# An FFT convolution and an MLP on one core: row-tiled second DFT stage, an in-place product, data as weights in the inverse, layer norm 2 inside the MLP

## The chip, the cores and the metric

The kernel runs on one core of a Trainium2 chip. A core has a matrix engine (TensorE, PE in the profile; its weight loads are listed apart as PEld), a vector engine (VectorE, DVE), a scalar engine (ScalarE, ACT), a general one (GpSimd, POOL) and a queue engine (SyncE, SP) that issues most transfers. Matmul results go to PSUM; ACT and DVE move them to SBUF. The metric is the device time of one execution in microseconds (us).

## The reference, cut to what matters

The sequence has S = 2048 tokens and D = 512 channels, all arrays are bf16.

```python
qn   = layernorm(q)                                   # over the channels
kv   = (k convolved causally with 4 taps per channel) * v
y    = irfft(rfft(pad(kv)) * rfft(pad(ssm_k)))[:S]    # per channel, length 4096, float32
y    = bf16(y) + kv * ssm_D                           # skip term per channel
h    = q + qn * y                                     # gate
out  = h + relu(layernorm(h) @ w1) @ w2               # w1: 512 x 1376, w2: 1376 x 512
```

The long convolution is the costly part beside the MLP. With the padded transform the kernel computes odd frequencies alone, with two stages of DFT matrices (32 values of `k1`, then 64).

## The kernel before, in words

The order on every engine is that of the program text (`manual_schedule`); the waits follow from the tiles that an instruction reads and writes. Tiles live in pools, and a pool that takes over the place of another waits for it.

**Setup (L94 to L192).** SP loads the filter `sk`, then `kT` and `vT` in four chunks each with transposing DMAs (L110 to L113), so that channels lie on partitions. POOL and DVE make integer phases, and ACT makes sine tables of them (`_sin`, `table`): `cc`, `cs` and, by POOL, `cn` = -`cs`. These hold the second stage's DFT matrices of all 32 `k1` as 128 x 128 blocks in which two 64 x 64 blocks stand on the diagonal and the rest is zero.

**Stage 1 (`stage1`).** `to_rows` (L195) turns the time axis to the partitions with PE transposes. Then, for eight groups `gb` of channels, 64 pairs of a matmul with the high and the low part of the first stage's matrix run on four row groups of 32 partitions, and ACT and DVE copy the four results. For the filter (L268), two `taps` (L255: four matmuls against diagonal weights, and a DVE product with `vT`) follow each `gb`. For the data (L292, `wide=True`) most matmuls have 128 columns, of which 64 meet zeros. A pool of eight PSUM buffers serves all of these.

**Stage 2 (`stage2`, L226).** For each `k1`, four matmuls of 256 columns in fp32r, with the DFT block as weights. For the filter (L283) DVE adds `ssm_D` to the real part and ACT copies the imaginary part into `kf`.

**Product (L308 to L340).** For each of 16 pairs `kp` of `k1`, `product` runs stage 2 on the data into PSUM, ACT copies columns 176 to 255 to SBUF for POOL, and DVE and POOL multiply by both parts of `kf` (L321). Two steps later `finish` adds the four partial products with matmuls against +1 and -1 on the diagonal (L331), and ACT writes the sums over `kf` (L333).

**Inverse stage 1 (L389).** 64 steps `m`, each with two matmuls (L394) whose weights are 128 columns of the data in `kf` and whose 256 moving columns are `dre`/`dim`. In between `ec_turns` and `ec_sins` make the table `ecore`.

**Inverse stage 2 (`inv2`, L412).** For each quarter `q` of the tokens 128 small matmuls (L421) on 16 tiles of 32 x 32, weights from the table, data moving, in full fp32 (the trace has two instructions for each). ACT copies the result to `zt`.

**Layer norms, gate, MLP (L428 to L526).** `ln1(q)` normalizes the input tokens (`xh`); `gate` multiplies with `zt`, adds, and takes the statistics for layer norm 2; `hln_` applies it; `transposes` turns the result on PE, and ACT copies it to `hlnT` (L473). `mlp1(sc)` makes 44 matmuls (L485) of 512 columns with relu on ACT, `mlp2(sc)` 44 more (L498); DVE adds the residual (L501), and SP stores.

Of the kernel before, what the change touches and what calls it, by code (L numbers as in the profile page):

```python
# [15 lines left out]
P = 128  # L16
# [40 lines left out]
def kernel(  # L57
# [28 lines left out]
    slotA = pl.push("slotA")  # L86
    vp = pl.push("vp")
    early = pl.push("early")
    wp = pl.push("wp", side="right")
    kvp = pl.push("kvp", side="right")  # L90
# [7 lines left out]
    dtab = consts.tile([P, DC, 64], BF16, name="dtab")  # L98
    for dp in range(2):
        src = bass.AP(tensor=A_ssm_D.tensor, offset=A_ssm_D.offset + 64 * dp, ap=[[0, 64], [P, DC], [1, 64]])  # L100
        nc.scalar.dma_start(out=dtab[64 * dp:64 * dp + 64, :, :], in_=src)
    vT = vp.tile([P, DC, S], BF16, name="vT")
    CH = 512
    kT = [(kvp if c < 2 else early).tile([P, DC, CH + 16], BF16, name=f"kT{c}") for c in range(4)]
    wdiag = kvp.tile([P, DC, KS, P], BF16, name="wdiag")
# [15 lines left out]
    eps_t = consts.tile([P, 1], F32, name="eps_t")  # L121
    nc.vector.memset(eps_t[:], EPS)

    hsc = consts.tile([P, 2], F32, name="hsc")
    hbi = consts.tile([P, 2], F32, name="hbi")
    for t_, v_ in ((hsc, TURN / 8192), (hbi, -0.5 * TURN)):
        nc.vector.memset(t_[:], 0.0)
        for dp in range(2):
            nc.vector.memset(t_[halves[dp], dp:dp + 1], v_)
# [6 lines left out]
    n1i = early.tile([P, 1], I32, name="n1i")  # L136
    for s in range(0, P, 32):
        nc.gpsimd.iota(n1i[s:s + 32, :], pattern=[[0, 1]], base=0, channel_multiplier=1)
    r1 = early.tile([P, 32], I32, name="f1_r")
    nc.gpsimd.iota(r1[:], pattern=[[2, 32]], base=1, channel_multiplier=0)  # L140
    n2i = early.tile([P, 1], I32, name="n2i")
    for s in range(0, P, 64):
        nc.gpsimd.iota(n2i[s:s + 64, :], pattern=[[0, 1]], base=0, channel_multiplier=1)
    r2 = early.tile([P, 32, 64], I32, name="w_r")
    nc.gpsimd.iota(r2[:], pattern=[[2, 32], [128, 64]], base=1, channel_multiplier=0)
    r3 = early.tile([P, 64], I32, name="dm_r")
# [6 lines left out]
    n1c = early.tile([P, 1], F32, name="n1c")  # L153
    n2c = early.tile([P, 1], F32, name="n2c")
# [3 lines left out]
    t1 = early.tile([P, 64], I32, name="f1_t")  # L158
    _turns(nc, t1[:, 0:32], r1[:], n1c[:], 128, True)
    _turns(nc, t1[:, 32:64], r1[:], n1c[:], 128, False)  # L160
    f1f = early.tile([P, 64], F32, name="f1_f")
# [4 lines left out]
    cc = wp.tile([P, 32, P], F32R, name="c2c")  # L166
    cs = wp.tile([P, 32, P], F32R, name="c2s")
    cn = wp.tile([P, 32, P], F32R, name="c2n")
    tsn = early.tile([P, 32, 64], I32, name="w_ts")
    _turns(nc, tsn[:], r2[:], n2c[:], 8192, False)  # L170

    def table(dst, turns):
        for dp in range(2):
            nc.scalar.activation(out=dst[:, :, 64 * dp:64 * dp + 64], in_=turns[:], func=ACT.Sin,  # L174
                                 scale=hsc[:, dp:dp + 1], bias=hbi[:, dp:dp + 1])

    table(cs, tsn)
    f1hi = consts.tile([P, P], BF16, name="f1_hi")
    f1lo = consts.tile([P, P], BF16, name="f1_lo")
    for f in (f1hi, f1lo):  # L180
        nc.gpsimd.memset(f[:, 64:128], 0.0)
    nc.vector.tensor_copy(out=f1hi[:, 0:64], in_=f1f[:])
    f1d = early.tile([P, 64], F32, name="f1_d")
    nc.vector.tensor_tensor(out=f1d[:], in0=f1f[:], in1=f1hi[:, 0:64], op=ALU.subtract)
    nc.vector.tensor_copy(out=f1lo[:, 0:64], in_=f1d[:])
    _turns(nc, r2[:], r2[:], n2c[:], 8192, True)
    for rg in range(DC):
        nc.gpsimd.tensor_tensor(out=wdiag[:, rg, :, :], in0=ident[:].unsqueeze(1).to_broadcast([P, KS, P]),
                                in1=wsh[:, rg, :].unsqueeze(2).to_broadcast([P, KS, P]), op=ALU.mult)
    for h in range(4):  # L190
        hs = slice(8 * h, 8 * h + 8)
        nc.gpsimd.tensor_single_scalar(out=cn[:, hs, :], in_=cs[:, hs, :].bitcast(F32), scalar=-1.0, op=ALU.mult)  # L192


# [6 lines left out]
    def copy(eng, o, i):  # L201
        if eng == "A":
            nc.scalar.copy(out=o, in_=i)  # L203
        else:
            nc.vector.tensor_copy(out=o, in_=i)

    def stage1(fl, a_out, engs, between=None, wide=False):

        for gb in range(8):
            pss = [psum.tile([P, 8, 64], F32, tag="ps", name=f"ps1_{r}") for r in range(4)]  # L210
            for gi in range(8):
                for f, first in ((f1hi, True), (f1lo, False)):
                    for rg in range(4):
                        rows = slice(32 * rg, 32 * rg + 32)
                        w = 2 if wide and gi < 7 else 1
                        nc.tensor.matmul(out=pss[rg][:, gi:gi + w, :].rearrange("p g c -> p (g c)"),  # L216
                                         lhsT=fl[rows, 8 * gb + gi, :, :].rearrange("p d n -> p (d n)"),
                                         rhs=f[rows, 0:64 * w], start=first, stop=not first,
                                         tile_position=(32 * rg, 0), skip_group_check=wide)
            for rg in range(4):  # L220
                j0 = 64 * rg + 8 * gb
                copy(engs[(4 * gb + rg) % len(engs)], a_out[:, :, j0:j0 + 8], pss[rg][:].rearrange("p g c -> p c g"))
# [3 lines left out]
    def stage2(ps, a_in, kp, s):  # L226

# [55 lines left out]
    for kp in range(16):  # L283
        ks = slice(2 * kp, 2 * kp + 2)
        ps = [psum.tile([P, 2, 256], F32, tag="ps", name=f"ps2k{s}") for s in range(2)]
        for s in range(2):
            stage2(ps[s], a1k, kp, s)
# [47 lines left out]
    for kp in range(16):  # L335
        product(kp)
        if kp >= LAG:
            finish()
# [219 lines left out]
```

## Time and profile before

| | |
|---|---|
| time, median of three runs | 246.2 us (245.7 to 248.65) |
| span of the profiled execution | 244.7 us, first to last instruction |
| busy share | PE 86%, DVE 63%, PEld 59%, ACT 54%, POOL 27% |
| chain that ended last | PE 80%, ACT 9%, issue 4%, DMA 3%, DVE 2% |

The profile is that of one execution; the time of that very execution is not recorded apart, and the median lies 1.5 us above its span. A busy engine is one with an instruction in flight; matmuls overlap, so PE's busy share is no measure of how much of its peak it reaches. The chain names, step by step from the end, what the next instruction waited for. The granted clock is the share of TensorE's full clock; it was 0.968 in the mean.

### The profile page before, as it was taken

What the parts mean: (1) busy time and instruction counts of PE and PEld (TensorE: products, weight loads), DVE (VectorE), ACT (ScalarE), POOL (GpSimd) and SP (SyncE); (2) the same over time, 40 slices, a digit from 0 to 9 for tenths busy, and PEclk for the clock granted to TensorE, in tenths of its full rate; (3) what the DMA queues carried; (4) which work ended last, traced back from release to release, by engine and by line L of the source; (5) the groups of instructions that cost most, each with busy time, mean ns of one, the idle gap of its engine ahead of it and who ended that gap; (6) DMA issues with size and microseconds to landing.
All of it is one profiled execution on the core that took longest, in us unless ns stands there. A gap on an engine that the chain in (4) does not pass through costs nothing.

```text
span 244.7 us, 7171 instructions
## 1 busy us (share of the span) xinstructions
PE 209.5 (86%) x3088; PEld 144.7 (59%) x3104; DVE 153.1 (63%) x296; ACT 132.7 (54%) x232; POOL 65.3 (27%) x94
## 2 busy tenths in 40 slices
PE   0586998999857999989988786499999999999992
PEld 0573546999646999969975464334544544454440
DVE  7986987967636989959975778200247747751031
ACT  3878554666765888879943321636226136335500
POOL 6499600000004999971010221000002202200000
PEclk9999999999997999999999999559999999999998
DMA  6999910000000000039970000000110011012011
GB/s 211 302 202 168 144 34 3 4 0 0 5 3 5 1 0 0 3 74 209 279 250 3 5 5 5 0 0 0 30 48 11 0 44 46 0 34 56 0 43 43
DMA packets 23663, 13.88 MB, mean 57 GB/s; under 512 B 19056, under 2 KB 22480, under 8 KB 23504
## 3 DMA queue, kind: packets, MB, share of 16 engines
q1 hardware_dynamic: 22560, 13.36, 24.3%
q8 instruction: 24, 0.39, 0.7%
q10 hardware_dynamic: 1072, 0.07, 0.4%
q14 instruction: 7, 0.06, 0.1%
HBM read 7.08 MB, written 2.10 MB: 38 GB/s over the span
## 4 chain that ended last, share of the span: by engine, by line
PE 80%; ACT 9%; issue 4%; DMA 3%; DVE 2%; ACTq 0%
PE ps1m L485 17%; PE ps2m L498 15%; PE pz L421 9%; PE psi L394 6%; PE pst L198 5%; PE psy L331 5%; PE pkv L259 4%; PE ps L216 4%; PE u L231 4%; DMA sk<-in_A_ssm_k_dram 3%; PE u L233 3%; PE ps2k L233 3%; PE ps2k L231 3%; ACT a1x L203 2%; ACT c2c L174 2%
## 5 line engine op out<-in xcount | busy, mean ns | idle before, releaser
L485 PE MATMUL ps1m<-hlnT,w 128*128 128x512 bf16 (+1 forms) x175 | 41.2, 397 | 1.5 <-ACT hlnT L473 1.3
L487 ACT ACTIVATE h1T<-ps1m 128x512 bf16<-128x512 f32 (+1 forms) x44 | 26.2, 597 | 27.1 <-PE ps1m L485 27.1
L501 DVE TENSOR_TENSOR o<-ps2m,xh 128x512 bf16<-128x512 f32 x16 | 10.9, 690 | 47.9 <-PE ps2m L498 47.9
L498 PE MATMUL ps2m<-w,h1T 128*128 128x512 bf16 (+1 forms) x169 | 38.8, 379 | 0.4
L485 PEld LDWEIGHTS <-w 128*128 128x128 bf16 (+1 forms) x176 | 18.2, 104 | 24.0 <-issue 5.4
L321 DVE TENSOR_TENSOR t<-u,kf 128x704 fp32r<-128x704 f32 x32 | 26.8, 887 | 4.4 <-ACT usb L317 4.4
L321 POOL TENSOR_TENSOR t<-usb,kf 128x320 fp32r<-128x320 f32 x32 | 28.4, 927 | 3.0 <-ACT usb L317 2.4
L498 PEld LDWEIGHTS <-h1T 128*128 128x128 bf16 (+1 forms) x176 | 17.1, 98 | 20.0
L421 PE MATMUL pz<-bp,ecore 32*32 32x128 f32 x1024 | 22.0, 384 | 6.6 <-issue 5.7
L430 POOL TENSOR_SCALAR rstd<-mv 128x4 f32<-128x4 f32 x8 | 1.8, 229 | 92.2 <-DVE mv L437 92.2
L421 PEld LDWEIGHTS pz<-bp,ecore 32*32 32x32 f32 x1024 | 15.2, 103 | 13.2 <-issue 8.9
L425 ACT CAST zt<-pz 128x512 bf16<-128x512 f32 x16 | 8.2, 600 | 21.6 <-PE pz L421 21.6
L435 DVE BATCH_NORM_STATS2 st<-xh 128x6 f32<-128x512 bf16 x32 | 19.7, 683 | 0.0
L333 ACT CAST kf<-psy 128x512 fp32r<-128x512 f32 x32 | 18.4, 646 | 1.6
L394 PE MATMUL psi<-dre,kf 128*128 128x256 f32 x64 | 15.8, 287 | 0.8 <-ACT kf L333 0.8
L473 ACT COPY hlnT<-pt 128x1024 bf16<-128x1024 bf16 x8 | 7.7, 1015 | 15.0 <-PE pt L472 15.0
L331 PE MATMUL psy<-t,ipos 128*128 128x512 f32 x48 | 15.8, 390 | 0.0
L394 PE MATMUL psi<-dim,kf 128*128 128x256 f32 x64 | 15.4, 282 | 0.0
L259 PE MATMUL pkv<-kT,wdiag 128*128 128x512 bf16 x56 | 14.8, 381 | 0.4
L198 PE MATMUL pst<-ident,sk 128*128 128x128 bf16 x64 | 6.7, 295 | 9.1 <-DMA sk<-in_A_ssm_k_dram 9.1
L203 ACT CAST a1k<-ps 128x512 fp32r<-128x512 f32 x20 | 10.4, 593 | 7.1 <-PE ps L216 7.1
L289 ACT CAST kf<-ps2k 128x512 fp32r<-128x512 f32 x16 | 10.3, 641 | 5.4 <-PE ps2k L233 5.3
(107 smaller groups left out, 426.7 us busy)
## 6 DMA issues: line engine op xcount, KB each, us to landing
sk<-in_A_ssm_k_dram SPq DMA_DIRECT2D x1, 2048.0 KB, 8.3
xh<-in_A_q_dram SPq DMA_DIRECT2D x4, 512.0 KB, 8.4
out_dram<-o SPq DMA_DIRECT2D x64, 32.0 KB, 1.6
w<-in_B_w_dram SPq DMA_DIRECT2D x1, 1376.0 KB, 15.1
w<-in_B_w_dram SPq DMA_DIRECT2D x1, 1280.0 KB, 18.3
w<-in_B_w_dram SPq DMA_DIRECT2D x1, 96.0 KB, 17.9
dtab<-in_A_ssm_D_dram ACTq DMA_DIRECT2D x2, 32.0 KB, 8.3
kT<-in_A_k_dram SPq DMA_TRANSPOSE x4, 6.5
```

The lines of the kernel that those rows point to most:

```text
L198: nc.tensor.transpose(out=pst[:, i, :], in_=src[:, :, :, 8 * q + i], identity=ident[:])
L231: nc.tensor.matmul(out=ps[:, kk, :], lhsT=w_re[:, k1, :], rhs=a_in[:, k1, :], start=True, stop=False, skip_group_check=True)
L259: nc.tensor.matmul(out=ps[:], lhsT=wdiag[:, rg, j, :], rhs=kT[c][:, rg, 16 - j:CH + 16 - j], start=(j == 0), stop=(j == KS - 1))
L321: eng.tensor_tensor(out=t[:, :, j, :], in0=in0.unsqueeze(1).to_broadcast([P, 2, n, 2]), in1=kfr[:, :, j, ks], op=ALU.mult)
L331: nc.tensor.matmul(out=psy[:], lhsT=m_[:], rhs=t_.rearrange("p j k -> p (j k)"), start=first, stop=not first)
L333: nc.scalar.copy(out=kf[:, s, :, 2 * kp:2 * kp + 2], in_=psy[:].rearrange("p (j k) -> p j k", k=2))
L394: nc.tensor.matmul(out=ps[:, i, :], lhsT=kf[:, c, 4 * m:4 * m + 4, :].rearrange("p r k -> p (r k)"), rhs=d[:].rearrange("p a b -> p (a b)" ...
L421: nc.tensor.matmul(out=pz[32 * a:32 * a + 32, r4, l4, :], lhsT=ecore[rows, rho, n2, :], rhs=rhs, start=(rho == 0), stop=(rho == 1), tile_p ...
L435: nc.vector.bn_stats(out=st[:, i, :], in_=xh[:, 4 * q + i, :])
L485: nc.tensor.matmul(out=ps1[:fsz, :], lhsT=w1[:, c, fc * P:fc * P + fsz], rhs=hlnT[:, c, sc * SCW:(sc + 1) * SCW], start=(c == 0), stop=(c ...
L487: nc.scalar.activation(out=h1T[:fsz, fc, :], in_=ps1[:fsz, :], func=ACT.Relu)
L498: nc.tensor.matmul(out=ps2[:], lhsT=h1T[:ksz, fc, i * P:(i + 1) * P], rhs=w2[:ksz, fc, :], start=(fc == 0), stop=(fc == NFC - 1))
```

## The change

**Setup.** The tables become one tile `tab` of 64 x 64 blocks (sine, cosine, minus sine, minus cosine) on both halves of the partitions, without zeros: one ACT call each over 2048 elements, one ahead of the filter's transposes and three behind them. `cn` goes. `dsm` (four small loads), `sel` and `dx` are new; POOL makes `dx`.

**Stage 1.** The skip term is no longer added to `kf`: for the filter, `skip_term` begins each PSUM buffer with a matmul of two rows. The data's stage 1 is no longer widened and comes directly behind its transposes, ahead of stage 2 of the filter.

**Stage 2.** Each matmul takes a 64-row tile, with real and imaginary part together as 128 weight columns; the two halves of the partitions are two tiles (`tile_position`). The filter's result is copied over `a1k`.

**Product.** For the data both `u` and its rotation by 90 degrees are computed, so the complex product becomes two multiplications with the filter's values, written over `a1x` and `a1k`. DVE does 11 of 16 `kp` from PSUM, POOL five, for which ACT copies. The recombining matmuls go.

**Inverse stages.** Inverse stage 1 makes 16 steps `b` of 16 matmuls, 256 in all, each with 128 moving columns and 128 weight columns of data, and writes over `ax`. Inverse stage 2 takes the data as weights (32 rows, 128 columns) and 32 columns of the table as the moving part, in fp32r, so its result has channels on partitions.

**Layer norms and MLP.** The input and its normalized form are turned by transposing DMAs (`rows_T`), the gate works on the turned form, and its result feeds mlp1 directly. `w1c` is w1 less its column means, and the scale of layer norm 2 is applied with the residual on the output; `back` turns the gate's result back for the statistics and the residual.

The diff, cut to its core:

```diff
+    dsm = consts.tile([P, 64], BF16, name="dsm")
+    nc.gpsimd.memset(dsm[:], 0.0)
+    for rg in range(DC):
+        nc.scalar.dma_start(out=dsm[32 * rg:32 * rg + 2, :], in_=A_ssm_D[rg * P:(rg + 1) * P].rearrange("(d g) -> d g", d=2))
...
-    cc = wp.tile([P, 32, P], F32R, name="c2c")
-    cs = wp.tile([P, 32, P], F32R, name="c2s")
-    cn = wp.tile([P, 32, P], F32R, name="c2n")
+    tab = wp.tile([P, 32, 4, 64], F32R, name="tab")
...
+    nc.gpsimd.memset(dx[:], 0.0)
...
+    nc.gpsimd.tensor_copy(out=dx[:, :, 0:32], in_=dsm[:].unsqueeze(2).to_broadcast([P, 64, 32]))
+    _sin(tab[:, :, 0, :], tsn[:], 8192)
...
+    def skip_term(ps, rg, gb):
+        rows = slice(32 * rg, 32 * rg + 2)
+        nc.tensor.matmul(out=ps[:].rearrange("p g c -> p (g c)"), lhsT=sel[rows, :],
+                         rhs=dx[rows, 8 * gb:8 * gb + 8, :].rearrange("p g c -> p (g c)"),
+                         start=True, stop=False, tile_position=(32 * rg, 0), skip_group_check=True)
...
-    table(cc, r2)
+    _sin(tab[:, :, 1, :], r2[:], 8192)
+    _sin(tab[:, :, 2, :], tsn[:], 8192, neg=True)
+    _sin(tab[:, :, 3, :], r2[:], 8192, neg=True)
...
-    stage1(xfl, a1x, "ADADADAA", wide=True)
+    stage1(xfl, a1x, "ADADADAA")
...
+    prod = pl.push("prod", bufs=4, side="right")
+    psum = pl.push("psP", bufs=2, space=PSUM)
+    def stage2(ps, h, src, kp, w_re, w_im):
+        for kk in range(2):
+            k1 = 2 * kp + kk
+            for s, w in enumerate((w_re, w_im)):
+                for d in range(2):
+                    nc.tensor.matmul(out=ps[:, kk, d, h, :, :],
+                                     lhsT=tab[halves[d], k1, w:w + 2, :].rearrange("p a b -> p (a b)"),
+                                     rhs=src[halves[d], :, k1, s, :], start=(s == 0), stop=(s == 1),
+                                     tile_position=(64 * d, 0), skip_group_check=True)
...
+    for kq in range(8):
+        ps = psum.tile([P, 2, 2, 2, DC, 64], F32, tag="ps", name="psk")
+        for h in range(2):
+            stage2(ps, h, a1k, 2 * kq + h, 1, 0)
+        copy("A", pair(a1k, 2 * kq), half(ps, 0))
+        copy("D", pair(a1k, 2 * kq + 1), half(ps, 1))
+    for kp in range(16):
+        u = psum.tile([P, 2, 2, 2, DC, 64], F32, tag="ps", name="u")
+        stage2(u, 0, a1x, kp, 1, 0)
+        stage2(u, 1, a1x, kp, 2, 1)
+        eng, us = nc.vector, [half(u, 0), half(u, 1)]
+        if kp % 3 == 1:
+            eng = nc.gpsimd
+            for h in range(2):
+                usb = prod.tile([P, 4, DC, 64], F32, tag="usb", name="usb")
+                nc.scalar.copy(out=usb[:], in_=us[h])
+                us[h] = usb[:]
+        for h, dst in enumerate((a1x, a1k)):
+            eng.tensor_tensor(out=pair(dst, kp), in0=us[h], in1=pair(a1k, kp).bitcast(F32), op=ALU.mult)
...
+    def inv1(b):
+        ps = psum.tile([P, 8, P], F32, tag="ps", name="psi1")
+        d, g0 = b // 8, 8 * (b % 8)
+        for g in range(8):
+            for src, r, first in ((ax, ra, True), (ak, rb, False)):
+                nc.tensor.matmul(out=ps[:, g, :], lhsT=src[:, :, d, g0 + g],
+                                 rhs=r[:].rearrange("p a b -> p (a b)"), start=first, stop=not first)
+        copy("A" if b % 4 != 3 else "D", ax[:, :, d, g0:g0 + 8], ps[:].rearrange("p g x -> p x g"))
...
+    def rows_T(dst, src):
+        nc.sync.dma_start_transpose(out=dst[:].rearrange("p i r t -> p (i r) t"), in_=src.rearrange("p i d -> p (i d)"))
...
+    def inv2(q, pool):
+        pz = pool.tile([P, DC, 4, P], F32, tag="pz", name="pz")
+        for i in range(4):
+            for a in range(4):
+                n2 = 16 * a + 4 * q + i
+                for rho in range(2):
+                    for rg in range(DC):
+                        rows = slice(32 * rg, 32 * rg + 32)
+                        nc.tensor.matmul(out=pz[:, rg, i, 32 * a:32 * a + 32],
+                                         lhsT=ax[rows, 64 * rho + n2, :, :].rearrange("p d g -> p (d g)"),
+                                         rhs=ecore[rows, rho, n2, :], start=(rho == 0), stop=(rho == 1),
+                                         tile_position=(32 * rg, 0), skip_group_check=True)
+        return pz
+
+    def gate(q, pz):
+        for r in range(DC):
+            nc.vector.tensor_tensor(out=qT[q][:, :, r, :], in0=pz[:, r, :, :], in1=qT[q][:, :, r, :], op=ALU.mult)
+        nc.vector.tensor_tensor(out=xT[q][:], in0=qT[q][:], in1=xT[q][:], op=ALU.add)
+        hT[q] = xT[q]
+
+    def back(q):
+        nc.sync.dma_start_transpose(out=xh[:, 4 * q:4 * q + 4, :].rearrange("p i (r c) -> p (i r) c", r=DC),
+                                    in_=hT[q][:].rearrange("p i r t -> p (i r t)"))
...
-            nc.vector.tensor_tensor(out=o[:], in0=ps2[:], in1=xh[:, t, :], op=ALU.add)
+            nc.vector.scalar_tensor_tensor(out=o[:], in0=ps2[:], scalar=rstd2[:, t, :], in1=xh[:, t, :],
+                                           op0=ALU.mult, op1=ALU.add)
...
+    FS = 344
+    for n in range(DFF // FS):
+        fs = slice(n * FS, (n + 1) * FS)
+        pm = psB.tile([P, 512], F32, tag=f"pm{n}", name="pm")
+        for c in range(DC):
+            nc.tensor.matmul(out=pm[:, 0:FS], lhsT=ones[:], rhs=w1[:, c, fs], start=(c == 0), stop=(c == DC - 1))
+        nc.vector.tensor_tensor(out=w1c[:, :, fs], in0=w1[:, :, fs],
+                                in1=pm[:, 0:FS].unsqueeze(1).to_broadcast([P, DC, FS]), op=ALU.subtract)
+    pz0 = inv2(0, psA)
+    gate(0, pz0)
+    back(0)
...
+    pz1 = inv2(1, psB)
+    gate(1, pz1)
+    back(1)
+    pl.pop("psA")
+    psum = pl.push("psM", bufs=4, space=PSUM)
+    ln1(2)
+    stats(xh[:, 0:4, :], mv2, rstd2, 0)
+    mlp1(0)
+    pz = inv2(2, psB)
+    gate(2, pz)
+    back(2)
+    ln1(3)
+    mlp2(0)
+    stats(xh[:, 4:8, :], mv2, rstd2, 1)
+    mlp1(1)
+    pz = inv2(3, psB)
+    gate(3, pz)
+    back(3)
+    mlp2(1)
+    stats(xh[:, 8:12, :], mv2, rstd2, 2)
+    mlp1(2)
+    mlp2(2)
+    stats(xh[:, 12:16, :], mv2, rstd2, 3)
+    mlp1(3)
+    mlp2(3)
```

## The prediction

> **What bounds the kernel now.** I read the chain that ended last first: TensorE (PE) has 80% of it, so I cut the span into stages and asked for each engine's busy time there (columns: stretch, length, then PE, weight loads PEld, DVE, ACT, POOL, the granted PE clock, DMA).
>
> ```profile
> 16.80:39.90 23.10, 19.63 (x568) 10.36 (x576) 19.53 (x32) 14.60 (x23) 11.73 (x14) 1.00 0.80 107
> 45.70:61.20 15.50, 15.50 (x134) 15.37 (x137) 11.86 (x17) 10.14 (x16) 0.00 (x0) 1.00 0.01 2
> 61.20:75.30 14.10, 9.13 (x513) 7.61 (x512) 7.85 (x13) 10.41 (x21) 0.79 (x2) 1.00 0.02 5
> 75.30:105.10 29.80, 29.37 (x183) 27.12 (x184) 25.62 (x31) 23.47 (x59) 27.05 (x31) 0.94 0.00 1
> 105.10:123.80 18.70, 17.85 (x135) 16.59 (x135) 15.72 (x30) 16.83 (x32) 4.68 (x11) 1.00 0.82 211
> 123.80:153.00 29.20, 22.57 (x1029) 15.53 (x1027) 21.21 (x61) 7.62 (x15) 4.71 (x8) 1.00 0.13 39
> 158.30:240.70 82.40, 81.11 (x392) 38.06 (x400) 32.17 (x80) 32.03 (x50) 5.03 (x8) 0.97 0.09 25
> ```
>
> These are: stage 1 of the filter with the taps; stage 2 of the filter; stage 1 of the data; the product; inverse stage 1; inverse stage 2; the MLP. PE fills all but the third. What the loss there is, the chain in order of time says (start, length, what): a table on ACT ahead of stage 1, and stalls called issue where many small matmuls run.
>
> ```profile
> 16.80 3.98 ACT c2c L174 x2
> ...
> 133.67 2.69 PE pz L421 x118
> 136.35 0.77 issue
> 137.12 2.74 PE pz L421 x112
> ```
>
> Then the groups by shape for prices (busy, mean ns of one, idle before), the first weight loads after a wait, and four stretches cut where the clock changed.
>
> ```profile
> L321 POOL TENSOR_TENSOR t<-usb,kf 128x320 fp32r<-128x320 f32 x32 | 28.4, 927 | 3.0 <-ACT usb L317 2.4
> L321 DVE TENSOR_TENSOR t<-u,kf 128x704 fp32r<-128x704 f32 x32 | 26.8, 887 | 4.4 <-ACT usb L317 4.4
> L198 PE MATMUL pst<-ident,vT 128*128 128x128 bf16 x64 | 5.9, 254 | 0.8 <-DVE vT L262 0.8
> L288 DVE TENSOR_TENSOR kf<-ps2k,dtab 128x512 fp32r<-128x512 f32 x16 | 11.0, 694 | 3.5 <-PE ps2k L233 3.4
> ```
> ```profile
> 108.35 0.19 PEld L394 LDWEIGHTS psi<-dre,kf 128*128 128x128 f32 x1 [1.28 <-ACT kf L333]
> 108.46 0.19 PEld L394 LDWEIGHTS psi<-dim,kf 128*128 128x128 f32 x1
> 108.58 0.19 PEld L394 LDWEIGHTS psi<-dre,kf 128*128 128x128 f32 x1
> ```
> ```profile
> 68.49:71.90 3.41, 2.39 (x128) 1.93 (x128) 1.89 (x3) 2.54 (x5) 0.00 (x0) 1.00 0.02 5
> 71.90:75.31 3.41, 1.47 (x100) 1.35 (x100) 1.89 (x3) 2.17 (x5) 0.79 (x2) 1.00 0.02 5
> 75.31:78.73 3.42, 3.00 (x14) 3.00 (x15) 1.37 (x2) 0.99 (x4) 1.32 (x2) 0.50 0.00 0
> ```
>
> A weight load of 128 fp32 columns holds the next back by 0.108 us (108.35 to 108.46). A 256-column fp32r matmul is paced at 0.118, so its load is hidden. The clock halved after a stretch in which PE was busy 43% (1.47 of 3.41), and not after 70%.
>
> **The change, along the time axis** (span times; the profiled span is 244.7 us, the median of the runs 246.2, so 1.5 lies around it).
>
> *To the end of stage 1 of the filter (39.9 before).* After the filter's transposes ACT computes three sine tables instead of two, 2.04 us each: PE waits 2.1 longer for ACT's first copy. That wait also covers POOL's new work: clearing `dx` (4096 elements, by 311 ns for 256 some 3.2 us) and its copy (2048 elements, 3 to 5 us between the 289 ns cast of 128 and the 2780 ns scale of 1024) end by 17 to 20 us, stage 1's second round starts at 23.6. The skip term adds per round four 512-column matmuls on four row groups. Four 64-column ones start every 0.03 us here, and a 512-column one takes 0.216 in the MLP, so four at once cost 0.22 and in turn 0.86; I take 0.22 (the nearest row is the same tiling): 8 x 0.22 = 1.8. PE now idles some 4 us in one piece, which leaves a 3.41 us stretch under 43% busy: one stretch at half clock in a PE-bound stage, 1.5. ACT's queue issues four small loads for `dsm` in place of two (0.5 to 0.9 each): its sine table load moves from 3.05 to 4.8 at most, ahead of the table's input at 7.2, so nothing. Sum +5.4: 45.3.
>
> *Stage 1 of the data.* Its transposes (5.9) end at 51.2. Before, stage 2 of the filter covered their last copy; now PE waits 1.3 for it. The widened matmuls go, but stage 1 issues as many instructions as before, and the issue stalls come each 3.4 to 3.5 us here as in inverse stage 2 (133.67 to 137.12), once per some 118 to 128 pairs. So PE keeps its 12.0 (61.24 to 73.2); below that, ACT's 20 copies of 0.535 set 10.7. End 64.7.
>
> *Stage 2 of the filter.* Block-diagonal weights with K=128 become two 64-row tiles: still 128 matmuls of 256 columns, but two at once: 16 per round in 8 x 0.118 = 0.95. DVE's copy of 1024 elements takes 1.22 (1225 ns in `to_rows`) and sets the pace: first data matmul 9.7 after the start, plus 2.0 for the last banks of stage 1 and a half-clock stretch, since that stage keeps PE under half busy. 76.4; the old order reached this point at 75.7.
>
> *Product.* Gone are 64 recombining matmuls (L331, 0.23 each) and 32 ACT copies (L333). PE needs 0.95 per `kp` where it needed 1.88 (8 x 0.118 and 4 x 0.23). But each `kp` now multiplies 2 x 1024 elements instead of splitting off 31% to POOL. From 694 (512) and 887 (704) DVE needs 1.2 each, 2.4 per `kp`, on 11 of 16. With two PSUM buffers, and the in-place write waiting for both halves' matmuls, DVE waits 1.2 once per three `kp`: 6.05 per three, 33.8 in all. POOL has 5 `kp` of 2 x (2.75 to 2.97, by 927 for 320) = 27.5 to 29.7, starts near 2.7 and catches up at kp 13: 33.0. So 33.8 against 33.1 before: no gain, the bound moves from PE to DVE and POOL. 110.2.
>
> *Inverse stage 1.* Before, 128 pairs of 256 columns. Now 256 pairs of 128 columns, whose weights are the data, 128 fp32 columns each, read with a stride. The matmul alone would be half of 0.118, 0.06; the load is then the longer half. Rows: 0.092 per pair for strided bf16 transposes (5.9/64), 0.108 for the first fp32 load, 0.118 in the stream. I take 0.108: 27.6, where the old stage took 15.4. ACT's 12 copies of 1.0 and sines of 5.9, and DVE's 23 us with two layer norms in it, fit beside. `xh` and w1 come in before this stage now, w2 goes out on ACT's queue after it and has 25 us until mlp2(0) (18 to land before). 137.9 = t0.
>
> *Between.* The mean of w1 (16 matmuls, 2.3) and four DVE subtractions from PSUM of 1376 elements (1.56 each) start at t0+1.5 and hold DVE until t0+8.4; inverse stage 2 for q=0 runs beside (128 pairs, four row groups at once, 32 x 0.108 = 3.5, where it took 6.9 per q). Gate 0 is 4 x 0.65 + 1.2: mlp1(0) starts at t0+12.2 = 150.1, against 158.3. I add 1.5 for a half-clock stretch. Gone from before it: L425's copies, the PE transposes, L473.
>
> *MLP.* 8 x 9.5 of matmuls (9.50 for 44) + 2 x 3.5 for q=2, 3 = 83.0. The new wait is DVE's gate 2 on `qT2`. SP issues back 0, back 1, `xT2`, `qT2` in turn; the row is `kT`/`vT`: 2.0 to 3.5 us of SP each, landing 3.1 apart and some 3.8 after the issue ends. norm 2 ends at t0+21.9, so `qT2` lands at about t0+28.5. Behind gate 2 on DVE stand layer norm 3 (5.7) and mlp2(0)'s four outputs; PE has filled the four PSUM buffers at t0+35 and gets one back at t0+38: 3. Layer norm 2's scale costs nothing (L501 becomes one operation of the same shape); its back transposes are hidden unless they take 10 us more.
>
> The Trainium skill's VectorE: DVE Perf Modes, section The three transpose paths, gives 1309 ns for a DMA transpose of 128x128 bf16. By it a call of 16 blocks would be an estimated 20.9 us, four in turn 84, and gate 2 some 55 us late. Here calls of that size land 3.1 apart.
>
> Sum: 150.1 + 1.5 + 83.0 + 3 = 237.6 for PE's end (240.7), tail 4.0 as now: span 241.6, time **243.1**, 1.3% less. What a measurement can tell from no change here is about 2%.
>
> **Rivals.**
> - *All loads hide well, the clock stays up*: transposes' pace 0.092 in inverse stage 1 (-4.1), no MLP stall (-3), no half-clock stretches (-4): 232. For it: PE stayed at 1.00 through the transposes. Against: it needs three things at once.
> - *Half clock where PE is half busy, slower than before.* In the product PE has 2.9 of 6.05 us, in inverse stage 1 a 0.06 matmul per 0.108. The two measured bounds are 43% (halved) and 70% (not). At half clock the first load took 0.17 (75.73 to 75.90): 256 x 0.062 = +15.9 if all of inverse stage 1, about +8 if half, and 0.95 per three `kp`, +2.5 for half the product: 253. A halved 3.41 us costs 1.2 there, so three of them undo the gain.
> - *Strided fp32 loads are dearer*: for bf16 a strided load lasts 202 ns, a contiguous one 98. An extra 0.05 per pair is +13: 256.
> - *The row tiles do not overlap*: 16 matmuls per round in 1.9: stage 2 of the filter +5.5, product +5, skip +5: 258. Against: stage 1's four per 0.03.
>
> The skill's TensorE: Matmul & The Clock Gate, Part 1, lets the clock fall after an idle window of about 3.4 us. No stretch here is idle that long, so by it the second rival costs nothing; the row above, halved after 43% busy, speaks against that.
>
> **Numbers.** Forecast case (239 to 248) 0.45, the fast rival 0.20, half clock 0.17, dear loads 0.10, no overlap 0.08. The range takes most of all but the last, 230 to 258. Faster by over 2% (below 241.3): the fast rival and a third of the forecast case, 0.35. Slower by over 2% (above 251.1): most of the last three, 0.30. Within: 0.35.
>
> **What would show it.** Product of 33 to 35 us with DVE and POOL both near full; inverse stage 1 with PEld starts 0.1 apart; PE's issue stalls still in stage 1; DVE idle before gate 2, released by the DMA of `qT2`; one PE wait of 2 to 4 us before mlp1(1). Wrong it would be by a load pace away from 0.108, half clock in the long middle, or transposes from SBUF that land later than those from DRAM.

## The result, and the profile after

The changed kernel takes **289.3 us** (287.1 to 293.6) where the kernel before took 246.9 in the same session: ratio 1.166, interval 1.158 to 1.175. The forecast was 243.1 with a range up to 258. The span of the profiled execution is 287.0 us (244.7 before) and the mean granted PE clock 0.77 (0.97 before).

The stretches of the changed kernel's span, cut at its stages (columns as in the prediction: stretch, length, then busy time of PE, weight loads PEld, DVE, ACT, POOL, then the granted PE clock and DMA):

```profile
19.50:44.10 24.60, 23.26 (x600) 11.86 (x607) 18.89 (x31) 13.78 (x23) 1.45 (x3) 0.89 0.41 74
51.50:64.10 12.60, 8.83 (x512) 7.33 (x512) 7.83 (x12) 10.36 (x20) 0.00 (x0) 0.53 0.02 5
64.10:80.20 16.10, 12.43 (x128) 11.03 (x128) 8.57 (x7) 7.66 (x9) 0.00 (x0) 0.74 0.89 220
80.20:118.30 38.10, 23.11 (x256) 20.86 (x256) 27.67 (x24) 10.09 (x11) 25.08 (x17) 0.76 0.03 7
118.30:175.10 56.80, 56.73 (x256) 56.59 (x256) 18.78 (x43) 17.06 (x20) 4.80 (x7) 0.50 0.18 34
175.10:191.90 16.80, 15.44 (x274) 12.90 (x274) 11.01 (x10) 0.00 (x0) 0.00 (x0) 0.60 0.40 107
191.90:282.50 90.60, 89.93 (x604) 44.16 (x608) 40.90 (x87) 26.25 (x44) 7.59 (x12) 0.92 0.34 64
```

These are stage 1 of the filter, stage 1 of the data, stage 2 of the filter, the product, inverse stage 1, the way to `mlp1(0)`, and the MLP. One row stands out: inverse stage 1, 56.8 us, in which PE and its loads are busy throughout and the clock is 0.50. The same stage took 16.0 us before.

Where the 42.3 us of span came from, by stage:

| stage | before, us | after, us | difference | running sum | end forecast | end measured |
|---|---|---|---|---|---|---|
| start to end of filter stage 1 | 39.9 | 44.1 | +4.2 | +4.2 | 45.3 | 44.1 |
| data stage 1 and filter stage 2, to the first matmul of `u` | 35.8 | 36.1 | +0.3 | +4.5 | 76.4 | 80.2 |
| product | 32.7 | 38.1 | +5.4 | +9.9 | 110.2 | 118.3 |
| inverse stage 1 | 16.0 | 56.8 | +40.8 | +50.7 | 137.9 | 175.1 |
| from there to `mlp1(0)` | 33.9 | 16.7 | -17.2 | +33.5 | 151.6 | 191.8 |
| MLP | 81.7 | 90.6 | +8.9 | +42.4 | 237.6 | 282.4 |
| tail | 4.7 | 4.6 | -0.1 | +42.3 | 241.6 | 287.0 |

The MLP ends here with PE's last matmul, and the forecast's 151.6 is its 150.1 with the 1.5 that it adds for half clock.

Inverse stage 2 does what the change says: half of the path to `mlp1(0)` is gone. That saving is lost more than twice over in inverse stage 1. The weight loads there, in order of time (start, length), first of the changed kernel, then of the kernel before:

```profile
129.80 0.32 PEld L399 LDWEIGHTS psi<-ra,a1x 128*128 128x128 f32 x1
130.02 0.31 PEld L399 LDWEIGHTS psi<-rb,a1k 128*128 128x128 f32 x1
130.24 0.31 PEld L399 LDWEIGHTS psi<-ra,a1x 128*128 128x128 f32 x1
```
```profile
115.06 0.19 PEld L394 LDWEIGHTS psi<-dre,kf 128*128 128x128 f32 x1
115.18 0.19 PEld L394 LDWEIGHTS psi<-dim,kf 128*128 128x128 f32 x1
115.30 0.19 PEld L394 LDWEIGHTS psi<-dre,kf 128*128 128x128 f32 x1
```

A pair of a load and its matmul starts every 0.22 us where one started every 0.12, and there are 256 instead of 128. So the question is the 0.22. Two things differ from the stage before: the clock is halved, and the 128 words of a load stand 512 bytes apart.

### The profile page after: what moved, and what is told of

Read it like the earlier page. It is cut to its first block, busy times and chain, and to the rows that moved or that the text cites. A ratio compares the mean times of both kernels' runs of the same rounds, so it can differ in the third digit from the quotient of the medians.

```text
span 287.0 us, 6258 instructions
## 1 busy us (share of the span) xinstructions
PE 242.5 (85%) x2756; PEld 177.4 (62%) x2768; DVE 156.7 (55%) x243; ACT 99.7 (35%) x138; POOL 57.0 (20%) x66
## 4 chain that ended last, share of the span: by engine, by line
PE 74%; DVE 13%; ACT 4%; POOL 3%; issue 3%; DMA 2%; ACTq 0%; POOLq 0%
PE psi L399 20%; PE ps2m L474 15%; PE ps1m L463 14%; PE pz L438 7%; PE pkv L252 5%; DVE a1k L317 5%; DVE a1x L317 5%; PE ps L209 3%; PE u L288 3%; PE psk L288 3%; DMA dsm<-in_A_ssm_D_dram 2%; ACT a1x L188 2%; DVE a1k L190 2%; PE pst L195 2%; POOL wdiag L180 2%
## 5 line engine op out<-in xcount | busy, mean ns | idle before, releaser
L399 PE MATMUL psi<-ra,a1x 128*128 128x128 f32 x128 | 54.2, 423 | 3.4 <-DVE k1o L342 3.4
L399 PE MATMUL psi<-rb,a1k 128*128 128x128 f32 x128 | 54.2, 423 | 0.0
L399 PEld LDWEIGHTS psi<-ra,a1x 128*128 128x128 f32 x128 | 40.2, 314 | 3.6 <-POOL ec_r L347 3.6
L463 PE MATMUL ps1m<-xT,w1c 128*128 128x512 bf16 (+1 forms) x176 | 40.5, 391 | 0.0
L399 PEld LDWEIGHTS psi<-rb,a1k 128*128 128x128 f32 x128 | 40.2, 314 | 0.0
L288 PE MATMUL u<-a1x,tab 64*128 64x256 f32 x256 | 23.1, 339 | 12.3 <-DVE a1k L317 11.2
L463 PEld LDWEIGHTS <-w1c 128*128 128x128 bf16 (+1 forms) x176 | 18.0, 103 | 21.7 <-issue 2.5
L288 PEld LDWEIGHTS u<-a1x,tab 64*128 64x128 f32 x256 | 20.9, 239 | 14.5 <-issue 11.1
L477 DVE SCALAR_TENSOR_TENSOR o<-ps2m,rstd,xh 128x512 bf16<-128x512 f32 x16 | 11.8, 749 | 32.7 <-PE ps2m L474 32.7
L438 PEld LDWEIGHTS pz<-ecore,a1x 32*128 32x128 f32 x512 | 18.9, 234 | 1.4 <-issue 1.0
L438 PE MATMUL pz<-ecore,a1x 32*128 32x32 f32 x512 | 19.2, 296 | 0.0
```

What stands on the lines that cost most here:

```text
L288: nc.tensor.matmul(out=ps[:, kk, d, h, :, :], lhsT=tab[halves[d], k1, w:w + 2, :].rearrange("p a b -> p (a b)"), rhs=src[halves[d], :, k1, ...
L399: nc.tensor.matmul(out=ps[:, g, :], lhsT=src[:, :, d, g0 + g], rhs=r[:].rearrange("p a b -> p (a b)"), start=first, stop=not first)
L438: nc.tensor.matmul(out=pz[:, rg, i, 32 * a:32 * a + 32], lhsT=ax[rows, 64 * rho + n2, :, :].rearrange("p d g -> p (d g)"), rhs=ecore[rows, ...
L463: nc.tensor.matmul(out=ps1[:fsz, :].rearrange("p (i t) -> p i t", i=4), lhsT=w1c[:, c, fc * P:fc * P + fsz], rhs=hT[sc][:, :, c, :], start ...
L477: nc.vector.scalar_tensor_tensor(out=o[:], in0=ps2[:], scalar=rstd2[:, t, :], in1=xh[:, t, :], op0=ALU.mult, op1=ALU.add)
```

## The experiments

**Theory A**: the clock is halved because 128 moving columns keep the array streaming for too little of the time, and a load goes with the clock. **Theory B**: a load of fp32 words that stand apart takes 0.22 by itself. **C**: something else in the stage.

**1. More moving columns.** `rz` holds zeros, then `ra` or `rb`, so that 12 of 16 matmuls have 256 columns:

```diff
-                nc.tensor.matmul(out=ps[:, g, :], lhsT=src[:, :, d, g0 + g], rhs=r...
+            w = 1 if g % 4 == 3 else 2
+                nc.tensor.matmul(out=ps[:, g:g + w, :], lhsT=src[:, :, d, g0 + g], rhs=r...  # 128 * w columns
```

> The changed kernel, with 256 moving columns in 12 of 16 matmuls of each step of inverse stage 1, of which 128 meet zeros (dsm and sel move to another pool for room). Theory A (the clock is halved because the array streams in under half of the time: 128 of 266 cycles per pair; the load itself takes 266 cycles of whatever clock is granted): clock 1.0 within two or three of its 3.41 us stretches, 0.118 us per pair, the stage falls from 56.8 to 30 to 36 us, and what follows is warmer by 2 to 5; span 287 to 253 to 262. Rival B (a strided fp32 load takes 0.22 us by itself and the clock is only a companion): pairs stay at 0.22, stage 56 to 58, span 285 to 289. Rival C (the clock is low for another reason, such as heat or the stages ahead): clock stays 0.5, pairs 0.22 to 0.23.

Measured: 288.3, ratio 1.168 (1.161 to 1.175), as without the edit. Its stretches of inverse stage 1, cut where the clock changed:

```profile
111.00:124.60 13.60, 9.19 (x57) 8.95 (x57) 9.26 (x14) 2.92 (x3) 7.71 (x11) 0.50 0.18 40
124.60:176.50 51.90, 51.89 (x233) 51.75 (x233) 15.30 (x35) 16.15 (x19) 3.13 (x5) 1.00 0.14 31
```

The clock is back at 1.00 for 52 us, and 233 pairs still take 0.223 each. So the halved clock is not needed for 0.22: theory A doesn't hold as the only cause.

**2. Neighbouring words, in place.** The weights are 128 words in a row of the same two tiles:

```diff
-lhsT=src[:, :, d, g0 + g]
+lhsT=src[:, P // 2 * d + g0 + g, :, :].rearrange("p s g -> p (s g)")
```

> The changed kernel with the weights of inverse stage 1 read as 128 neighbouring words instead of words 512 bytes apart; the right data are left out of that stage, the number and shape of its matmuls are unchanged. Theory A: nothing changes, 0.22 us per pair at half clock, stage 56 to 57 us. Rival B: 0.11 to 0.12 per pair, stage 28 to 31 us, whatever the clock.

Measured: 313.4 in its one run, span 311.6. The edit adds a wait of its own: a step now reads words that the step before has just written, so each waits for a copy:

```profile
PEld psi L399 <- ACT a1x L188: 15.6, 12, 1.4
PE psi L399 <- ACT a1x L188: 13.4, 12, 1.2
```

(the waits between 120 and 200 us: total, times, longest). Within a step the loads start 0.213 apart at half clock. It separates nothing, except that a load in line isn't faster than 0.213 at half clock.

**3. Neighbouring words that nothing writes, with 256 columns.** Both weights come from `a1k`, which this stage only reads:

```diff
-lhsT=src[:, :, d, g0 + g]                       # kernel of experiment 1
+lhsT=ak[:, 64 * d + g0 + g].rearrange("p s g -> p (s g)")
```

> The changed kernel with 256 moving columns (as in e1_wide_inv1) and with the weights of both matmuls of inverse stage 1 taken as 128 neighbouring words of `a1k`, which nothing writes in this stage. It leaves the right data out of inverse stage 1 (the product's first half isn't read, and the words are in another order), so the output isn't the reference's; the number and size of the instructions stay. Theory B (a load whose 128 words stand 512 bytes apart takes 0.22 by itself): a load and matmul take 0.118 at the full clock, as in the kernel before; 256 of them 30 us, and the time 288 - 27 = 261. Theory C (something else of this stage, its copies or its instruction supply, sets 0.22): the stage stays at 57 us and the time at 288.

Measured: 265.2, ratio 1.066 (1.059 to 1.073).

```profile
119.60:124.90 5.30, 5.27 (x25) 5.30 (x26) 3.48 (x8) 1.02 (x1) 1.67 (x2) 0.50 0.19 43
124.90:151.90 27.00, 27.00 (x233) 26.86 (x232) 15.13 (x35) 15.67 (x19) 3.13 (x5) 1.00 0.32 59
```

With the words in line, 0.116 per pair at the full clock instead of 0.223. Both loads also read `a1k` alone here, where experiment 1 reads `a1x` and `a1k` in turn; that isn't the cause, since the steps of experiment 5 that read `a1k` alone at 128 words take 0.223 again. Theory B holds, C falls.

**4. Neighbouring words, with the 128 columns of the change.**

> The same neighbouring words of `a1k` as weights, with the 128 moving columns of the changed kernel; it leaves the same data out. If a load sets the pace and the clock doesn't matter: 0.11 per matmul, 28 us for the stage, time 260. If the clock stays halved because the array streams for less than half of the time, and a load goes with the clock, as the 0.213 of e2_contig_weights suggests: 0.213 per matmul, 55 us, time 286 to 289, with a stretch of half clock of over 50 us in the stage.

Measured: 288.0, ratio 1.156 (1.147 to 1.164).

```profile
119.30:174.20 54.90, 54.84 (x256) 54.69 (x256) 18.79 (x43) 17.08 (x20) 4.96 (x8) 0.50 0.20 38
```

0.214 per pair, at half clock for the whole stage. So the halved clock is a cause as well: each of the two, distance and halved clock, is enough for 0.21 to 0.22, and they don't add. This is why mending one of them alone (experiments 1 and 4) moves nothing, and both together the 24 us between 289.3 and 265.2.

**5. Which distances cost.** Experiment 1 with another distance in each step:

```diff
+    STRIDE = (128, 128, 1, 2, 4, 8, 16, 32, 64, 128, 127, 120, 96, 1, 128, 1)
...
+        return ak.rearrange("p k s g -> p (k s g)")[:, 0:P * s].rearrange("p (j s) -> p j s", s=s)[:, :, g % s]
```

> The kernel of e1_wide_inv1, with weights that are read from `a1k` at another distance in each of the 16 steps of inverse stage 1: 128, 128, 1, 2, 4, 8, 16, 32, 64, 128, 127, 120, 96, 1, 128, 1 words between neighbouring columns. It leaves the right data out of the stage. If any distance other than one word costs (B1): 1.9 us per step of 16 matmuls at 1, and 3.5 at all others. If only a distance that is a large power of two costs (B2): 3.5 at 128 and perhaps 64, 1.9 at 127, 120 and 96 and below 32. If the price grows with the distance (B3): steps between 1.9 and 3.5, and 127 like 128.

Measured: 282.6 in one run. PE alone, one row per step, for the distances 1, 2, 4, 8, 16 and 127 words (stretch, length, PE busy, clock):

```profile
125.91:127.76 1.85, 1.85 (x18) 1.00 0.00 0
127.77:129.68 1.91, 1.91 (x19) 1.00 0.00 0
129.69:133.40 3.71, 3.71 (x19) 1.00 0.00 0
133.41:137.27 3.86, 3.86 (x18) 1.00 0.00 0
137.28:140.82 3.54, 3.54 (x17) 1.00 0.30 69
151.55:155.26 3.71, 3.71 (x18) 1.00 0.28 63
```

None of the three forms fits whole. Two words (8 bytes) are nearly as good as one, and from four words (16 bytes) on the step takes its full 3.5 to 3.9, at 127 as at 128: neither "any distance", nor "powers of two", nor a slow growth.

**6. Does bf16 pay it too?** More rungs, in fp32 and in bf16 with weights from `xh`.

> The ladder of e7_stride_ladder again, with other rungs: steps in fp32 at 128, 128, 3, 5, 1 and 128 words, and steps in bf16 whose weights come from `xh` at 1, 2, 4, 6, 8, 16, 32, 64, 63 and 3 elements (moving columns from `w1`, so the right data is left out of these steps). e7_stride_ladder had 1.9 us per step of 16 matmuls up to 2 fp32 words (8 bytes) and 3.5 to 3.9 from 4 words (16 bytes) on. If the distance in bytes decides (S1): bf16 at 4 elements (8 bytes) still 1.9 us, at 8 (16 bytes) and beyond 3.5 or more. If the distance in elements decides (S2): bf16 1.9 us at 2 and 3.5 already at 4. If bf16 hides it, because a bf16 load is shorter (S3): 1.7 to 1.9 us at all distances; the trace of before has a bf16 load with matmul at 0.202 where the weights stand 128 bytes apart, against 0.098 in line, which speaks against S3.

Measured: 267.3 in one run. The steps of bf16 at 1, 4 and 64 elements, then fp32 at 3 and at 5 words (stretch, length, PE and PEld busy, clock, DMA):

```profile
125.21:126.75 1.54, 1.54 (x17) 1.41 (x18) 1.00 0.00 0
128.29:129.82 1.53, 1.53 (x19) 1.53 (x17) 1.00 0.00 0
136.06:137.76 1.70, 1.70 (x19) 1.70 (x18) 1.00 0.00 0
139.30:142.12 2.82, 2.82 (x19) 2.82 (x18) 1.00 1.25 280
142.12:145.73 3.61, 3.61 (x18) 3.61 (x18) 1.00 0.07 15
```

In bf16 the matmuls set the pace at every distance (0.109 for 256 columns, 0.056 for 128), up to 0.16 us more per step at 64 elements. So neither bytes nor elements as such decide (S3): where 12 of 16 matmuls have 256 moving columns, a scattered bf16 load is hidden nearly whole, and an fp32 one is not. fp32 at three words lies between, 0.175.

**7. The same scatter in the kernel before.**

```diff
-lhsT=kf[:, c, 4 * m:4 * m + 4, :].rearrange("p r k -> p (r k)")
+lhsT=kff[:, :, 2 * m + c]        # kff: kf as 128 rows of 128 words
```

> The kernel before, with the weights of its inverse stage 1 read from `kf` as 128 words 512 bytes apart, and nothing else changed; the right data is left out of that stage. Theory B: 128 matmuls of 256 columns at 0.22 take 28 us instead of 15.4, and the time is 247 + 13 = 260, ratio 1.05. If a distance between the words costs only in the changed kernel's surroundings: 247, ratio 1.00.

Measured: ratio 1.041 (1.031 to 1.051). Inverse stage 1 in that kernel, and in the kernel before:

```profile
107.60:136.50 28.90, 28.83 (x128) 28.63 (x128) 16.18 (x30) 15.97 (x28) 2.75 (x4) 1.00 0.64 171
```
```profile
108.35:124.40 16.05, 16.00 (x128) 15.50 (x128) 14.98 (x29) 14.26 (x27) 2.74 (x4) 1.00 0.99 258
```

12.9 us more in the stage, at the full clock, for the place of the words alone; the whole span grows by 10.8, from 244.7 to 255.5.

**8. What holds the clock down.** In experiments 1 and 4 the array streams about half of the time. This is an estimate from experiment 6, where bf16 matmuls of 256 and of 128 columns follow each other at 0.109 and 0.056. By it a step of experiment 1, with 12 matmuls of 256 columns and 4 of 128, streams 1.53 of its 3.57 us, 43% (the 48% of the expectation counts all 16 as wide); experiment 4, at half clock, streams 0.112 of each 0.214, 52%. Yet the clock stayed up in the one and down in the other. So this run starts wide and goes on narrow:

```diff
-            w = 1 if g % 4 == 3 else 2           # kernel of experiment 3
+            w = 1 if g % 4 == 3 or b >= 6 else 2
```

> The kernel of e5_contig_wide (it leaves the same data out), with 256 moving columns only in the first 6 of the 16 steps of inverse stage 1 and 128 in the last 10, all with neighbouring words as weights. In e1_wide_inv1 the array streamed 0.107 of each 0.22 at the full clock, 48%, and the clock stayed up; in e6_contig_narrow it streamed 0.107 of each 0.213 at half clock, 50%, and the clock stayed down. If a stretch about half busy keeps the clock that it is entered with (K1): the narrow steps run at the full clock, 0.11 per matmul, 10 steps in 18 us, and the time is 258 to 262. If narrow columns bring the clock down whatever it was (K2): after 3 to 10 us it falls, the narrow steps take up to 0.213, 30 us and more, and the time is 270 to 276.

Measured: 264.9 in one run. The first steps, the rest of the wide ones, and the ten narrow steps:

```profile
118.80:125.00 6.20, 6.15 (x31) 6.18 (x32) 3.47 (x8) 1.01 (x1) 1.67 (x2) 0.55 0.17 38
125.00:132.40 7.40, 7.40 (x66) 7.40 (x66) 3.25 (x6) 4.28 (x5) 0.00 (x0) 1.00 0.00 0
132.40:150.50 18.10, 18.10 (x163) 18.00 (x162) 11.88 (x30) 11.26 (x14) 3.13 (x5) 1.00 0.48 78
```

The narrow steps run at the full clock to the end, 0.112 per pair, where the same instructions took 0.214 at half clock in experiment 4. K1 holds for this stage: streaming about half of the time, it keeps the clock that it is entered with. Of theory A there remains that 128 columns don't raise a halved clock; they don't bring a full one down. PE counts as busy throughout in both runs, so its busy share doesn't tell the two apart, and what measure the clock follows isn't shown. Nor is it shown that the changed kernel would keep a full clock: there, by the same estimate, its scattered loads would let the array stream a quarter of the time (0.056 of 0.223). The changed kernel enters inverse stage 1 after a product in which PE was busy 23.1 of 38.1 us, with the clock already down.

**9 to 11. Stage 2 of the filter.** It took 16.1 us where 11.7 were forecast (the expectations' 17.8 goes on to the product's first multiplication). Its waits in the changed kernel:

```profile
ACT a1k L188 <- PE psk L288: 8.4, 8, 2.2
DVE a1k L190 <- ACT a1k L188: 8.4, 8, 3.7
```

DVE's copy of a round waits for ACT's copy of the same round, eight times. First try: each half of a round in banks of its own within the tile (`out=ps[:, h, d, kk, :, :]` for `out=ps[:, kk, d, h, :, :]`).

> The changed kernel with the two halves of each stage 2 result in PSUM banks of their own. Theory A2 (ACT's and DVE's copies of one round run one after the other only because both halves lie in the same banks): DVE no longer waits for ACT in stage 2 of the filter, which falls from 17.8 to 11 to 13 us; the product changes by less than 2; span lower by 4 to 8. Rival B2 (they are in turn because both write a1k, or the PE is late): the wait of DVE on ACT stays at 8 us, span within 1.

Measured: ratio 1.178 (1.170 to 1.185), with the same 8.4 us of waits. Second try, the halves in two tiles:

```diff
-        ps = psum.tile([P, 2, 2, 2, DC, 64], F32, tag="ps", name="psk")
+        pa = psum.tile([P, 2, 2, 2, DC, 64], F32, tag="ps", name="psk")
+        pb = psum.tile([P, 2, 2, 2, DC, 64], F32, tag="ps", name="psk")
```

> The changed kernel, with the two halves of a round of filter stage 2 in two PSUM tiles of the same buffers (each half used), so that ACT's copy and DVE's copy of one round read different tiles. If the two copies run in turn because they read one tile (D1): they run side by side, a round takes the longer of DVE's 1.23 and the matmuls' 1.0 to 1.7, and the stage 11 to 13 us instead of 17.8. If they run in turn because both write `a1k` (D2): the wait of DVE for ACT stays at 8.4 us, and the stage at 17 to 18.

Measured: 290.5 in one run, and these waits:

```profile
DVE a1k L190 <- PE psk L288: 9.6, 8, 2.6
ACT a1k L188 <- PE psk L288: 8.9, 8, 1.9
PEld psk L288 <- DVE a1k L190: 4.5, 6, 1.1
```

DVE no longer waits for ACT, so the turn came from the tile that both read, not from `a1k`, which both still write: by its waits this is D1. But the stage isn't shorter (17.6 us from its first matmul to its last, where the changed kernel has 15.4): with two buffers for two halves nothing is double buffered, and each copy alternates with its own matmuls. Third try, four tiles of half the size:

```diff
+            ps = psum.tile([P, 2, 2, DC, 64], F32, tag="ps", name="psk")     # in a pool of 4
+            stage2(ps, None, a1k, 2 * kq + h, 1, 0)                          # one half each
```

> The changed kernel with four PSUM tiles of half the size in filter stage 2: one copy per tile, ACT's and DVE's from different tiles, and each half double buffered. If the turn of the two copies is what made the stage 17.8 us instead of 11.7 (E1): a round takes the longer of DVE's 1.22 and the matmuls' 1.0 (2.1 at half clock), and the stage 11 to 13 us with the wait for the last copies of stage 1; the time falls by 3 to 6. If the halved clock in it is what counts (E2): matmuls of 2.1 per round, 15 to 17 us.

Measured: 287.1 in one run. The stage (from the last matmul before it), the product and inverse stage 1 in that run:

```profile
63.20:76.20 13.00, 10.29 (x131) 9.47 (x128) 9.93 (x9) 9.13 (x10) 0.00 (x0) 0.82 0.91 205
76.20:113.20 37.00, 21.70 (x256) 19.67 (x257) 26.54 (x23) 9.64 (x10) 25.07 (x17) 0.80 0.10 31
113.20:170.00 56.80, 56.75 (x256) 56.59 (x256) 18.78 (x43) 17.08 (x20) 4.81 (x7) 0.50 0.18 34
```

Its 128 matmuls take 10.3 us from first to last instead of 15.4, and the first matmul of `u` starts at 76.3 instead of 80.2. E1 holds: the turn of the two copies was the cost. Inverse stage 1 then ends 5.1 us earlier (170.0 for 175.1), but the span is only 1.7 shorter: the half clock that began at 105.4 lasted until 194.1 this time, over the whole way to `mlp1(0)` and beyond.

**12. The start.** POOL's clearing of `dx` goes to the head of DVE's list.

> The changed kernel, with the clearing of `dx` (3.51 us on POOL) put at the head of DVE's list. If POOL's clearing is what held DVE's multiplication of `w_r` (4.68 us instead of 1.28) and, with it in POOL's list, the first skip matmul: the multiplication takes 1.3, PE begins filter stage 1 some 3 us earlier (16.5 instead of 19.5), and the stage ends near 41.5 instead of 44.1. If DVE is held by the size of its own instruction or by POOL's other work: 4.7 stays, and the stage ends at 43 to 44.

Measured: 286.9 in one run. DVE's multiplication of `w_r` in the changed kernel beside POOL's clearing, and in this run:

```profile
8.03 4.68 DVE L44 TENSOR_SCALAR w_r<-w_r,n2c 128x2048 int32<-128x2048 int32 x1
```
```profile
8.12 3.51 POOL L178 MEMSET dx<- 128x4096 bf16 x1
```
```profile
8.04 1.28 DVE L44 TENSOR_SCALAR w_r<-w_r,n2c 128x2048 int32<-128x2048 int32 x1
```

POOL's clearing held DVE for its 3.5 us. PE began filter stage 1 at 16.4 instead of 19.5, as expected, but ended it at 42.6 instead of 43.4: most of the gain was lost, because PE then waits 3.0 us for ACT's first copy, which stands behind three sine tables that run until 22.3, and its third round starts at 26.6 instead of 27.3. The Trainium skill's SBUF — State Buffer, section SBUF: two separate sides, calls the port pair that DVE (in some of its modes) shares with GpSimd an exclusive lock, which the one that starts first holds for its whole instruction while the other is blocked. A hold of that length fits: 3.51 and 1.28 make 4.79, near the 4.68. By the records, though, DVE's instruction began first, at 8.03 against 8.12, so which of the two took the lock first isn't settled here.

**13. Could the kernel before gain from a held clock?** It has two stretches at half clock (from 75.3 and 153.8). Useless matmuls of 512 columns were put there: 8 after the data's stage 1, 10 and 8 around the first transposes of the last stage.

> The kernel before, with 8 matmuls of no use behind stage 1 of the data and 10 and 8 around the first transposes of the last stage, where PE waits and the clock halved after a stretch of 43% and 46% busy. Theory A (the clock follows how much of a 3.41 us stretch PE works): no half clock at 75 to 79 and less at 154 to 164, time lower by 2 to 5 us of 246.9 (1 to 2%). If the clock does not follow that: the same time or up to 2 us more.

Measured: ratio 1.0017 (0.9984 to 1.005). The stretch at 75 is gone, and the end of inverse stage 1 came at 123.9 instead of 124.4; but the second stretch stayed (149.9, 10.2 us), and the fillers there, at half clock themselves, put the first transposes of the last stage off from 155.1 to 159.0. No gain.

No version found beats the kernel before. The nearest, experiments 3 and 8 at a span of 263, leave the data out; to do it rightly, the words of a load would have to stand at most 8 bytes apart both for inverse stage 1 and for inverse stage 2, which reads the same tiles along the other index. No run tried that, and with inverse stage 1 in line and at the full clock experiment 3 is still 1.066 of the kernel before.

## Why the prediction was wrong

The span came out 45.4 us above the forecast, 287.0 against 241.6. By the prediction's own steps:

- **Inverse stage 1: forecast 27.7, measured 56.8, +29.1.** This is the step that failed. The term is the pace per pair, 0.108, which was read from two loads of the kernel before whose words stand in a row. Experiment 8 shows that price right for what it was taken from: 0.112 in line at the full clock, with 128 moving columns. But the words of the changed kernel's loads stand 512 bytes apart, which costs 0.223 at the full clock (1, 5, 7), and it enters the stage at half clock, at which even loads in line cost 0.214 (4). The prediction had both as rivals, each as an addition of some size: "strided fp32 loads are dearer" with 0.05 per pair (measured 0.11), and "half clock" with 0.062 per pair (measured 0.10). The mechanisms were right, their sizes half of the truth, and the two were taken as separate cases when both came. The 0.05 was set from the one row of scattered loads that there was, a bf16 load of 202 ns against 98 in line. That row itself has 0.104 between the two, close to the 0.11 measured for fp32; the prediction took half of it and gave no reason.
- **Stage 2 of the filter: forecast 11.7, measured 16.1, +4.4.** The price of DVE's copy was right (1.22). Wrong was that it would be the only pace: ACT's and DVE's copies were taken as running side by side, and they run in turn, because they read one tile. With a tile for each the eight rounds took 10.3, near the forecast's 9.7 (9 to 11).
- **Product: forecast 33.8, measured 38.1, +4.3.** DVE's 1.22 per multiplication is as priced, and POOL's 2.39 lower than the 2.75 to 2.97. The row tiles do overlap: 16 matmuls of `u` take 1.2 us at the full clock. At half clock they take 2.1, and the clock is down for half of the product (0.76). Once it has begun, DVE waits five times for PE, 9.6 us in all: 1.39 each at the full clock, and 2.26 in the three cases at half clock. These three cost 2.6 more, which stood in the half-clock rival, at 2.5. The other 1.7 is in waits of 1.39, and 1.6 ahead of the first multiplication, where the forecast had 1.2.
- **From there to `mlp1(0)`: forecast 13.7 with its half-clock stretch, measured 16.7, +3.0.** The path is another one: the forecast had `mlp1(0)` wait for DVE's gate 0, with inverse stage 2 hidden beside it. Gate 0 ends at 189.0, but PE itself is busy until 191.88, at a clock of 0.60 rather than one short stretch, and the chain that ended last runs through it (start, length, what):

```profile
176.48 4.74 PE pm L487 x16
181.23 10.65 PE pz L438 x173
191.88 11.41 PE ps1m L463 x44
```

- **MLP: forecast 86.0, measured 90.6, +4.6.** The stall at gate 2 that the forecast put at 3 did not come: DVE's gate starts at 208.02, as inverse stage 2 for q=2 ends, released by PE, not by the DMA. Instead the MLP meets half clock three times. `mlp1(0)` takes 11.5 and the first two `mlp2` 12.0 and 11.4 where an undisturbed one takes 9.7, which is 5.8; inverse stage 2 for q=2 takes 4.8 instead of 3.7.
- **Filter stage 1: forecast 45.3, measured 44.1, -1.2.** The skip matmuls are as priced, 0.22 to 0.23 per round at the full clock and 0.4 in the first two rounds, at half clock. That the sum is near is partly luck: POOL was not covered by ACT's wait, as the forecast had it; the first skip matmul waited for POOL's `dx` until 19.5.
- **Stage 1 of the data, with its transposes: forecast 19.4, measured 20.0.** The forecast's terms (5.9, 1.3 and 12.0) add to 19.2; its 64.7 is 0.2 too late.
- **Tail: forecast 4.0, measured 4.6.** The 4.0 counts from 240.7, where DVE's last instruction in the kernel before ends; its last matmul ends at 240.0, which makes 4.7 as after the change.

The rest adds to -1.2 + 0.6 + 0.6 = 0, so the error is 29.1 + 4.4 + 4.3 + 3.0 + 4.6 = 45.4.

Of the rule on the clock that the prediction weighed, that it falls after an idle window, this case keeps the prediction's own row (halved after 43% busy) and adds to it: PE is never idle in inverse stage 1, and yet the clock stays at half through that stage of experiment 4. The Trainium skill's TensorE: Matmul & The Clock Gate, section LDWEIGHTS, prices a load by its columns alone, P / 1.2, that is 107 ns for 128. Loads in line at the full clock agree (0.112). Scattered fp32 loads do not (0.223), nor do loads in line at half clock (0.213), and the measurement decides.

## What to carry to other kernels

When data becomes the stationary operand, ask how far apart the words of one load stand: in fp32, 8 bytes were nearly free here, 16 bytes or more about doubled the load, and matmuls of 256 columns didn't cover it. Price a stage with the clock that the stage before it leaves behind: here a stage in which the array streams about half of the time kept the clock it found, and a short wide start, with its loads in line, raised it for the rest of the stage. Two causes that each set the same pace hide one another; an edit that removes one and changes nothing doesn't clear it.

## What the runs showed of the hardware

- An fp32 load of 128 columns with its matmul, at the full clock: 0.116 at a distance of 1 word, 0.120 at 2, 0.175 at 3, 0.23 to 0.24 at 4, 8, 120 and 127, 0.223 to 0.226 at 5, 16, 32, 64, 96 and 128 (5 to 7). At half clock 0.213 in line and 0.221 at 128 words: scattered loads hardly depend on the clock.
- At about half streaming (43 to 52%, an estimate) the clock kept either value: it stayed at 1.00 for 18 us (8) and 52 us (1), and at 0.50 for 55 us (4).
- One POOL clearing of 3.51 us made a DVE instruction on another tile take 4.68 us instead of 1.28 (12).
- Copies by ACT and DVE from one PSUM tile ran in turn, also from different banks of it (9), and no longer waited for each other with two tiles (10, 11). The turn is a wait for a semaphore, which the program sets by tiles; that the engines couldn't read one tile at once isn't shown.
